# The queue that issues MoE 1's stores of the parts of x

## The chip, the cores and the metric

One Trainium2 chip, one core. The metric is the device time of one execution in microseconds (us), taken as the median over runs. The profile is one further execution, recorded by the hardware profiler; all times of day in the text are us from the start of its span.

## What is computed

The reference runs three layers in float32 on 2304 tokens of 512 features:

```python
attn_out = _attn_ref(**attn_kwargs)                  # attention with a memory term
x = attn_out.transpose(0, 2, 1, 3).reshape(2304, 512)
x = (silu(x @ w_gate) * (x @ w_val)) @ w_out         # MoE 1, d_ff = 1536
logits = x @ w_gate2; P = sinkhorn(exp(logits))      # MoE 2, 8 experts of 1024
out = sum_e P[:, e] * (relu(x @ w1[e]) @ w2[e])
```

The kernel makes each float32 product out of three products of float32r halves (high by high, high by low, low by high), and in MoE 2 and in part of MoE 1 it replaces eight block products by seven (Strassen-Winograd), which needs sums of blocks of x beside the blocks themselves.

## The kernel before

Time runs through attention (to about 340 us), MoE 1 (to about 670 us) and MoE 2 (to the end). MoE 1 takes the tokens in chunks of 512, 512, 512, 512 and 256. Chunks 0 and 1 go first; chunks 2 and 3 then go through their gates together in seven block products per slice of d_ff (`unit_gates`, L1045, called from the loop at L883, the "gate stage" below, from 424 to 587 us); from 587 to 670 us the last product of chunk 3 and all of chunk 4 follow (loop at L955, the "last stage").

As soon as a chunk of MoE 1's output stands in `x` (buffer name `xacc`), its seven parts for MoE 2 (four blocks and the sums T1 to T4) are made and kept in HBM, since MoE 2 reads each part again for every unit of weights. `parts` (L731) lists the seven, `parts_of` (L704) makes one in three steps, spread over three turns of a generator: ScalarE casts the block to its high half (L717, into a tile `xl`), VectorE subtracts to get the low half into the same tile (L720), and a DMA stores the tile of 512 KB to `xp` (L723). There are two `xl` tiles in the pool (L858), so the cast of part n+2 waits until the store of part n has landed. The chunk's logits (L670) use the same two tiles (cast L681, subtraction L683).

The parts of pairs 0 and 1 are made in the gate stage, those of pair 2 in the last stage, each time as work "aside" that the loop pulls one step at a time (`on`, L774). The parts of pair 3 and of the last 256 tokens are made in MoE 2's first microseconds (`last_parts`, L1460). Pair p has the stores xp_64 to xp_70 (p = 0), xp_71 to xp_77 (p = 1), xp_78 to xp_84 (p = 2).

All other DMAs run from the sync engine's queue (SP): in the gate stage per slice 1 MB of gate weights (`gw`, L654), 512 KB of output weights (`ws`, L654), two loads of 256 KB for the sums of weights (`hf`, L1025) and one store of 256 KB (`kh`, L899).

In the gate stage the seven products of a slice share PSUM tiles: `pc` accumulates four of them in a row, and between them ScalarE must copy the running value out (L1062, `hf<-pc`) before TensorE may add the next product. Between those products TensorE has two others (`pt`) and pieces of the output product of an earlier slice (`po`, spread by PIECES, L113).

The order in which each engine's instructions stand is set by the scheduling layer when the program is built: it walks through all instructions by readiness, so an instruction that is put on another queue changes the order around it on other engines too. Within its engine's queue an instruction is taken strictly in order, and what waits at the head holds all behind it.

Of the kernel before, what the change touches and what calls it, by code (L numbers as in the profile page):

```python
# [114 lines left out]
PAIRS2 = 4  # L115
# [17 lines left out]
def f32(ap):  # L133
    return ap.bitcast(F32)
# [26 lines left out]
class Kernel:  # L161
# [438 lines left out]
    def load_units(self):  # L600
# [14 lines left out]
        for n, (f, a) in enumerate(RAW):  # L615
# [5 lines left out]
            if a < 2:  # L621
                parts, kept = self.gw[f][:, :, a], self.keptg[f][:, :, a]
            else:
                self.ws[f] = self.wsp.tile([P, 2, 512], F32R, name="ws")
                parts, kept = self.ws[f], self.kepto[f]
# [15 lines left out]
            if a < 2:  # L641
                nc.sync.dma_start(self.keptw[f][:, a], w)
            nc.vector.tensor_sub(parts[:, 1], w, f32(parts[:, 0]))
            nc.sync.dma_start(kept, f32(parts))
            yield

# [54 lines left out]
        nc.vector.tensor_copy(sums, pl[:, :, 0])  # L701
        nc.vector.tensor_add(sums, sums, pl[:, :, 1])

    def parts_of(self, todo):  # L704


        nc, rest = self.nc, []
        for src, dst in [*todo, (None, None), (None, None)]:
            nxt = []
            for what in rest:  # L710
                nxt += what()
            rest = nxt
            if src is not None:
                src = src()
                t = self.xl.tile([P, 2, 512], F32R, name="xl")
                hi, lo = (t[:, n].rearrange("p (k t) -> p k t", k=2) for n in range(2))
                nc.scalar.copy(hi, src)  # L717

                def low(src=src, dst=dst, t=t, hi=hi, lo=lo):
                    nc.vector.tensor_sub(lo, src, f32(hi))  # L720

                    def store():
                        nc.sync.dma_start(dst, f32(t))  # L723
                        return []

                    return [store]

                rest.append(low)
            yield

    def parts(self, pair):  # L731

        t0, to = 2 * HT * pair, self.xparts[pair]
        q = {
            f"B{k + 1}{t + 1}": self.x[:, 2 * k:2 * k + 2, t0 + HT * t:t0 + HT * (t + 1)]
            for k in range(2) for t in range(2)
        }

        def total(name, a, b):
            def made():  # L740
                q[name] = self.tmpp.tile([P, 2, HT], F32, name="ws")
                self.nc.vector.tensor_sub(q[name], q[a], q[b])
                return q[name]

            return made

        plain = lambda name: lambda: q[name]
        yield from self.parts_of([
            (plain("B11"), to[0]), (total("T1", "B12", "B11"), to[3]), (total("T2", "B22", "T1"), to[2]),
            (plain("B21"), to[1]), (total("T3", "B22", "B12"), to[5]), (total("T4", "B21", "T2"), to[6]),  # L750
            (plain("B22"), to[4]),
        ])

    def moe1(self, last):


        nc, tc = self.nc, self.tc
        with ExitStack() as st, ExitStack() as waiting, ExitStack() as banks:
# [61 lines left out]
            def more(c, logits):  # L820
                t0, n = CHUNKS1[c]
                if logits:
                    yield from self.logits(pgv, "p0", self.xl, t0 // P, (t0 + n) // P)
                yield from self.parts(c)

            gws = self.stream(lambda: self.gwp, [P, 2, 2, 512], "gw", self.keptg * 2, 2)
            wss = self.stream(lambda: wsp0, [P, 2, 512], "ws", self.kepto * 2, 3)
# [31 lines left out]
            self.xwa_pool = ExitStack()  # L859
            self.xwa = pool("xwa", 3, self.xwa_pool)  # L860
            aside.append(more(0, True))


# [9 lines left out]
            for _ in ready:  # L873
                pass
            done(1, po)
            aside.append(more(1, False))


            banks.close()
            with ExitStack() as few:  # L880
                pc, pt = (pool(k, 2, few, space=PSUM) for k in ("pc1", "pt1"))
                po = new(n)
                for f in range(NF1):  # L883
                    weights(0, f)
                    todo = [(k, pend) for k in range(NK)] if f else []
# [29 lines left out]
            def both():  # L915

                steps = iter(lambda: next(self.prep0), 2)

                def behind():
                    while True:  # L920
                        with ExitStack() as order:
                            for ins in self.last_half:
                                order.enter_context(tc.issue_after(ins.ins))
                            if next(steps, self) is self:
                                return
                        yield

                weights0 = behind()
                for c in (1, 2):
                    t0, n = CHUNKS1[c]  # L930
                    for _ in self.logits(plog, "pl", self.xl, t0 // P, (t0 + n) // P):
                        yield next(weights0, None)
                for _ in self.parts(2):
                    yield next(weights0, None)
                for _ in weights0:
                    yield

            aside.append(both())
            h3p = pool("h3", 3, side="right")
            h3 = []  # L940
# [506 lines left out]
    def moe2(self):  # L1447
        nc, tc = self.nc, self.tc
        with ExitStack() as st:
# [9 lines left out]

            def last_parts():  # L1460

                yield from self.parts(PAIRS2 - 1)
                t0 = 2 * HT * PAIRS2
                yield from self.parts_of([
                    (lambda n=n: self.x[:, 2 * n:2 * n + 2, t0:NT], self.xparts[PAIRS2][n]) for n in range(2)
                ])

            def routing():
                for c in range(3, len(CHUNKS1)):
# [27 lines left out]
            right(0, 0)(0)  # L1497
            prep = self.prep0
            aside, pend, gate, nth = (last_parts(), routing()), [], 0, 0
            self.todo, self.now = [], 0  # L1500
            for u in range(UNITS):
# [110 lines left out]
```

## Time and profile before

| | |
|---|---|
| median of 3 runs | 2110.19 us (2109.23 to 2112.42) |
| the profiled execution | 2108.75 us, its span 2107.0 us |
| PE busy | 2065.8 us (98%) |
| DVE busy | 1718.9 us (82%) |
| ACT busy | 974.1 us (46%) |
| POOL busy | 523.0 us (25%) |
| DMA | 425.77 MB, mean 202 GB/s, all kernel transfers on one queue, q1 (59.9% of 16 engines' span) |

PE is TensorE, DVE is VectorE, ACT is ScalarE, SP the sync engine; `SPq` marks an instruction of SP's queue that issues a DMA. In a timeline row the bracket tells how long the engine stood idle before the row and what ended that. TensorE is the bound almost throughout, so what counts is where it stands idle; the page's slices show it below nine tenths only in the first.

### The profile page before, as it was taken

The numbers are of one execution on the slowest core, as the hardware profiler recorded it, in microseconds if no ns is written. First come the engines' busy times: TensorE is split into PE (matmuls) and PEld (weight loads), VectorE is DVE, ScalarE is ACT, GpSimd is POOL, SyncE is SP. The second block draws the span as 40 slices with busy tenths as digits, with TensorE's granted clock in tenths as the row PEclk, the third lists the DMA queues.
The fourth block names the chain that finished last, engine by engine and source line by source line (L and its number), as shares of the span: only waits on it lengthen the run. The fifth ranks groups of instructions, "written<-read, shape, count | busy, mean of one in ns | idle before, by whom it ended". The sixth has DMA issues, their size and how long they took to land.

```text
span 2107.0 us, 40598 instructions
## 1 busy us (share of the span) xinstructions
PE 2065.8 (98%) x15848; PEld 1904.7 (90%) x15848; DVE 1718.9 (82%) x3201; ACT 974.1 (46%) x1912; POOL 523.0 (25%) x458
## 2 busy tenths in 40 slices
PE   7999999999999999999999999999999999999999
PEld 5666787877889779999999999999999999999998
DVE  7899899674454578888888888988889888898887
ACT  7999543353333324444444444444444444444432
POOL 6888553000000032122121221212212122121210
PEclk9999999999999999999999999999999999999999
DMA  5342687375587837566475664755647556476564
GB/s 191 114 140 83 195 286 263 132 262 194 171 284 250 300 106 250 184 216 221 160 242 194 205 221 160 248 193 201 225 161 245 197 194 230 160 242 204 186 212 159
DMA packets 123359, 425.77 MB, mean 202 GB/s; under 512 B 13600, under 2 KB 13600, under 8 KB 120096
## 3 DMA queue, kind: packets, MB, share of 16 engines
q1 hardware_dynamic: 123168, 423.17, 59.9%
q8 instruction: 126, 2.06, 0.4%
q14 instruction: 65, 0.53, 0.1%
HBM read 374.36 MB, written 48.76 MB: 201 GB/s over the span
## 4 chain that ended last, share of the span: by engine, by line
PE 69%; DVE 11%; DMA 3%; issue 1%; ACT 1%; SPq 0%; DVEq 0%; ACTq 0%
PE pu L1433 16%; PE pc L1270 14%; PE pq L1433 11%; PE pt L1270 10%; PE po L546 5%; PE pt L1356 4%; PE p L546 3%; PE pc L546 3%; DVE m L1286 2%; DVE xacc L1439 2%; PE pt L546 2%; PE pq L546 2%; DMA xp<-xl 2%; DVE h L1255 1%; DVE h L1252 1%; DMA xr<-xp 1%
## 5 line engine op out<-in xcount | busy, mean ns | idle before, releaser
L1433 PE MATMUL pu<-xl,h 128*128 128x256 f32 x3240 | 424.8, 278 | 2.8 <-DVE xacc L1439 2.3
L1433 PEld LDWEIGHTS pu<-xl,h 128*128 128x128 f32 x3240 | 393.0, 188 | 7.2 <-DVE xacc L1439 4.0
L1270 PE MATMUL pc<-xr,w 128*128 128x256 f32 x3072 | 392.4, 277 | 4.9 <-DMA xr<-xp 3.4
L1270 PEld LDWEIGHTS pc<-xr,w 128*128 128x128 f32 x3072 | 369.1, 188 | 8.7 <-DMA xr<-xp 3.7
L1433 PE MATMUL pq<-xl,h 128*128 128x256 f32 x2430 | 316.9, 277 | 0.0
L1270 PE MATMUL pt<-xr,w 128*128 128x256 f32 x2304 | 294.1, 277 | 0.5 <-DMA xr<-xp 0.4
L1433 PEld LDWEIGHTS pq<-xl,h 128*128 128x128 f32 x2430 | 294.0, 188 | 0.3
L1254 ACT CAST h<-m 128x512 fp32r<-128x512 f32 (+1 forms) x345 | 190.3, 556 | 201.7 <-DVE m L1286 194.0
L1270 PEld LDWEIGHTS pt<-xr,w 128*128 128x128 f32 x2304 | 276.6, 188 | 1.8 <-issue 1.4
L1439 DVE SCALAR_TENSOR_TENSOR xacc<-pu,Pw,xacc 128x256 f32<-128x256 f32 x540 | 236.7, 474 | 38.7 <-PE pu L1433 38.6
L1277 ACT COPY m<-pc 128x512 f32<-128x512 f32 x192 | 112.1, 584 | 256.9 <-PE pc L1270 255.5
L1439 DVE SCALAR_TENSOR_TENSOR xacc<-pq,Pw,xacc 128x256 f32<-128x256 f32 x405 | 177.3, 473 | 47.1 <-PE pq L1433 47.1
L1255 DVE TENSOR_TENSOR h<-m,h 128x512 fp32r<-128x512 f32 (+1 forms) x345 | 207.0, 624 | 1.6
L1175 POOL TENSOR_TENSOR ws<-raw 128x512 f32<-128x512 f32 x60 | 80.8, 1358 | 502.7 <-DMA raw<-w 177.2
L1286 DVE SCALAR_TENSOR_TENSOR m<-m 128x512 f32<-128x512 f32 x240 | 187.0, 779 | 15.0 <-ACT m L1313 11.6
L1251 ACT ACTIVATE h<-m 128x512 fp32r<-128x512 f32 x192 | 121.4, 632 | 162.4 <-DVE m L1282 161.2
L1282 DVE TENSOR_TENSOR m<-pt,m 128x512 f32<-128x512 f32 x192 | 131.1, 683 | 57.5 <-ACT m L1277 51.4
L546 PE MATMUL p<-xs,gw 128*128 128x512 f32 (+1 forms) x864 | 171.0, 354 | 3.6 <-ACT hf L782 1.7
L546 PEld LDWEIGHTS p<-xs,gw 128*128 128x128 f32 x864 | 142.3, 188 | 30.7 <-DVE hf L783 2.8
L1252 DVE SCALAR_TENSOR_TENSOR h<-m,h 128x512 fp32r<-128x512 f32 x192 | 148.4, 773 | 7.6 <-ACT h L1251 7.2
L1162 POOL TENSOR_TENSOR w<-raw,w 128x512 fp32r<-128x512 f32 x15 | 38.6, 2574 | 435.3 <-ACT w L1161 435.3
L546 PE MATMUL po<-h,ws 128*128 128x512 f32 x576 | 144.6, 391 | 0.1
(229 smaller groups left out, 2943.0 us busy)
## 6 DMA issues: line engine op xcount, KB each, us to landing
xr<-xp SPq DMA_DIRECT2D x480, 512.0 KB, 4.1
raw<-w SPq DMA_DIRECT2D x64, 512.0 KB, 7.6
gw<-kg SPq DMA_DIRECT2D x24, 1024.0 KB, 7.1
graw<-gvo SPq DMA_DIRECT2D x36, 512.0 KB, 4.5
xp<-xl SPq DMA_DIRECT2D x30, 512.0 KB, 5.5
kg<-gw SPq DMA_DIRECT2D x24, 512.0 KB, 4.4
ws<-ko SPq DMA_DIRECT2D x24, 512.0 KB, 3.8
qk<-qkv SPq DMA_DIRECT2D x16, 640.0 KB, 4.9
```

The costliest lines, as they stand in the source:

```text
L546: self.nc.tensor.matmul(out, lhs[a], rhs[b], start=start and n == 0, stop=stop and n == 2, skip_group_check=shared)
L1251: nc.scalar.activation(hi, src, AF.Relu)
L1252: self.later(1, lambda: nc.vector.scalar_tensor_tensor(lo, src, 0.0, f32(hi), op0=ALU.max, op1=ALU.subtract))
L1254: nc.scalar.copy(hi, src)
L1255: self.later(1, lambda: nc.vector.tensor_sub(lo, src, f32(hi)))
L1270: self.marks[3] = nc.tensor.matmul(out[:, j * HT:(j + 1) * HT], w[:, a, j, k], x[:, b, k], start=start and j + k + n == 0, stop=k + n == 3 ...
L1277: self.marks[1] = nc.scalar.copy(t, src)
L1282: nc.vector.tensor_add(t, a, b)
L1286: relu = lambda out, a, b, op: nc.vector.scalar_tensor_tensor(out, a, 0.0, b, op0=ALU.max, op1=op)
L1356: nc.tensor.matmul(ph[:, j * HT:(j + 1) * HT], w[:, b, j, k], x[:, c, k], start=j + a + k + m == 0, stop=a + k + m == 4, skip_group_check= ...
L1433: nc.tensor.matmul(po[:, c], h[a][:, x, j, c * P:(c + 1) * P], w2[b][:, y, j], start=start and c + j + n == 0, stop=j + n == 3, skip_group ...
L1439: self.marks[2] = nc.vector.scalar_tensor_tensor(acc, po[:, c], self.Pw[:, at, e:e + 1], acc, op0=ALU.mult, op1=ALU.add)
```

## The change

`parts` and `parts_of` take the queue as an argument; MoE 1 passes ScalarE's, MoE 2 the sync engine's as before.

```diff
-    def parts_of(self, todo):
+    def parts_of(self, todo, queue):
...
                     def store():
-                        nc.sync.dma_start(dst, f32(t))
+                        queue.dma_start(dst, f32(t))
                         return []
...
-    def parts(self, pair):
+    def parts(self, pair, queue):
...
-        ])
+        ], queue)
...
-                yield from self.parts(c)
+                yield from self.parts(c, nc.scalar)
...
-                for _ in self.parts(2):
+                for _ in self.parts(2, nc.scalar):
...
-                yield from self.parts(PAIRS2 - 1)
+                yield from self.parts(PAIRS2 - 1, nc.sync)
...
-                ])
+                ], nc.sync)
```

21 of the 30 stores move (pairs 0 to 2), 9 stay (pair 3 and the last tokens). The orders of ACT, DVE, PE and SP differ in the gate stage's first 50 us, those of ACT, DVE and SP once more in the last stage; POOL's is the same.

ACT, second slice of the gate stage, before (L717 cast of a part, L802 cast of the gated values, L1062 copy of the running product, L1077 and L1088 the silu of the two token blocks):

```order
L717 CAST xl<-xacc 128x512
L1062 COPY hf<-pc 128x512
L717 CAST xl<-xacc 128x512
L802 CAST h<-sg 128x512
L1062 COPY hf<-pc 128x512
L1077 ACTIVATE sg<-hf 128x512
L717 CAST xl<-ws 128x512
L1062 COPY hf<-pc 128x512
```

The same place on ACT in the changed program:

```order
L717 CAST xl<-xacc 128x512
L723 DMA xp_70<-xl 128x1024
L723 DMA xp_68<-xl 128x1024
L802 CAST h<-sg 128x512
L1062 COPY hf<-pc 128x512
L717 CAST xl<-xacc 128x512
L717 CAST xl<-ws 128x512
L1077 ACTIVATE sg<-hf 128x512
L1062 COPY hf<-pc 128x512
L723 DMA xp_71<-xl 128x1024
L723 DMA xp_74<-xl 128x1024
L1062 COPY hf<-pc 128x512
```

Two stores now stand ahead of the cast and the copy, and the second copy stands behind both of the casts that wait for these two stores to land; before, one such cast stood between two copies.

ACT, third slice of the gate stage, in the changed program (L1040 casts the sums of weights, L681 the logits' blocks):

```order
L717 CAST xl<-ws 128x512
L1062 COPY hf<-pc 128x512
L1040 CAST ws<-ws 128x1024
L717 CAST xl<-ws 128x512
L723 DMA xp_76<-xl 128x1024
L1077 ACTIVATE sg<-hf 128x512
L723 DMA xp_77<-xl 128x1024
L717 CAST xl<-xacc 128x512
L1062 COPY hf<-pc 128x512
L723 DMA xp_75<-xl 128x1024
L1062 COPY hf<-pc 128x512
L681 CAST xl<-xacc 128x512 x2
```

The middle copy follows a cast that waits for xp_76, which was issued only three instructions earlier.

PE in that slice in the changed program (`pc<-xs,ws` is the second and the third product of the running sum, `pc<-ws` the fourth, and each of them waits for a copy L1062):

```order
L546 MATMUL pc<-xs,ws 128x512 x6
L546 MATMUL po_5317<-h,ws 128x512
L546 MATMUL po_5318<-h,ws 128x512 x2
L546 MATMUL po_5319<-h,ws 128x512 x2
L546 MATMUL po_5320<-h,ws 128x512 x2
L546 MATMUL pt<-xs,gw 128x512 x6
L546 MATMUL pc<-xs,ws 128x512 x6
L546 MATMUL pc<-ws 128x512 x6
```

Between the second product and the third TensorE has 13 other matmuls, between the third and the fourth none; before, there was one `po` piece or more between the third and the fourth in every slice but the first.

## Rows read from the trace of the kernel before

**Rows 1.** Busy time by stretch (us): PE, PEld, DVE, ACT, POOL; PEclk; DMA share; GB/s.

```profile
420.00:587.00 167.00, 162.54 (x709) 130.56 (x708) 95.16 (x165) 66.48 (x109) 1.53 (x2) 0.99 0.62 206
...
587.00:670.00 83.00, 83.00 (x561) 75.65 (x560) 38.08 (x73) 26.45 (x53) 0.00 (x0) 1.00 0.78 281
670.00:720.00 50.00, 45.00 (x304) 38.68 (x303) 31.44 (x54) 20.63 (x39) 0.00 (x0) 1.00 0.92 325
...
470.00:480.00 10.00, 6.91 (x29) 5.15 (x28) 4.21 (x10) 2.84 (x5) 0.00 (x0) 0.98 0.80 260
480.00:490.00 10.00, 10.00 (x39) 8.07 (x39) 5.95 (x11) 3.84 (x6) 0.00 (x0) 0.85 0.51 158
```

**Rows 2.** Timeline of the gate stage, PE: start, us, instruction, idle before it.

```profile
451.18 1.67 PE L546 MATMUL pc<-ws 128*128 128x512 f32 x6 [1.37 <-ACT hf L1062]
...
479.50 2.93 PE L546 MATMUL pc<-ws 128*128 128x512 f32 x6 [3.02 <-ACT hf L1062]
```

**Rows 3.** Timeline of the gate stage, ACT.

```profile
450.03 0.62 ACT L717 CAST xl<-ws 128x512 fp32r<-128x512 f32 x1 [3.51 <-DMA xp<-xl]
450.55 0.58 ACT L1062 COPY hf<-pc 128x512 f32<-128x512 f32 x1
...
478.35 0.62 ACT L681 CAST xl<-xacc 128x512 fp32r<-128x512 f32 x1 [6.05 <-DMA xp<-xl]
478.87 0.58 ACT L1062 COPY hf<-pc 128x512 f32<-128x512 f32 x1
```

**Rows 4.** The chain that ended last, gate stage: start, us, what.

```profile
468.29 10.04 DMA xp<-xl
...
487.31 1.36 PE pc L546 x6
```

**Rows 5.** Timeline of SP's queue at the slowest store.

```profile
465.73 0.32 SPq L654 DMA_DIRECT2D ws<-ko  x1
467.09 0.32 SPq L654 DMA_DIRECT2D gw<-kg  x1
468.29 0.32 SPq L723 DMA_DIRECT2D xp<-xl  x1
```

**Rows 6.** DMA view, 424 to 470 us: queue share; issues, KB each, median us to landing.

```profile
q1 hardware_dynamic: 3633, 12.33, 75.5%
...
xp<-xl SPq DMA_DIRECT2D x14, 512.0 KB, 3.7
```

**Rows 7.** The stores' line L723 over the whole span.

```profile
DMA to landing us min/median/max: 2.6/5.5/10.0
```

**Rows 8.** Groups by line, ACT, 420 to 587 us: busy us, mean ns, idle before.

```profile
L1062 ACT COPY hf<-pc 128x512 f32<-128x512 f32 x36 | 21.1, 587 | 55.4 <-PE pc L546 55.4
L1040 ACT CAST ws<-ws 128x1024 fp32r<-128x1024 f32 x12 | 12.6, 1053 | 15.8 <-PE pc L546 15.8
L1077 ACT ACTIVATE sg<-hf 128x512 f32<-128x512 f32 x12 | 7.6, 634 | 1.3 <-DVE hf L1067 0.7 <-DVE h L803 0.6
...
L717 ACT CAST xl<-ws 128x512 fp32r<-128x512 f32 x8 | 4.9, 619 | 5.9 <-DMA xp<-xl 3.5 <-PE p L698 2.4
```

**Rows 9.** Groups by line, 420 to 480 us, DVE's low halves.

```profile
L720 DVE TENSOR_TENSOR xl<-ws,xl 128x512 fp32r<-128x512 f32 x8 | 5.5, 684 | 2.8 <-ACT xl L717 2.8
```

**Rows 10.** DMA issues that touch xp: ns min/median/max, first and last start.

```profile
L1484 SPq DMA_DIRECT2D xr<-xp x480: 319/320/1336, 667.9 to 2074.8; - x160
L723 SPq DMA_DIRECT2D xp<-xl x30: 319/320/492, 424.6 to 712.0; - x30
```

**Rows 11.** Timeline of the last stage, ACT.

```profile
634.55 0.62 ACT L717 CAST xl<-ws 128x512 fp32r<-128x512 f32 x1 [2.67 <-DMA xp<-xl]
635.07 0.38 ACT L782 ACTIVATE sg<-p 128x256 f32<-128x256 f32 x1
```

**Rows 12.** Timeline of the last stage, PE.

```profile
630.98 3.10 PE L546 MATMUL p<-xs,gw 128*128 128x256 f32 x24
...
638.10 2.17 PE L546 MATMUL p<-xs,gw 128*128 128x256 f32 x17
```

## The prediction

> **What bounds the kernel now.** I read the page first (PE 98% busy), then the busy time by stretch, because a change to 21 stores can only matter where TensorE stands idle while they are made. The stores of pairs 0 and 1 lie in the gate stage, those of pair 2 in the last stage. In the gate stage PE is busy 162.54 of 167.00 us, so 4.46 us are idle [rows 1]. In the last stage it is busy 83.00 of 83.00 us: nothing to gain there [rows 1]. From 670 to 720 us it idles 5.00 us [rows 1], but those are MoE 2's first loads and the nine stores that stay on SP; the order there is the same in both programs, so I let it move along unchanged.
>
> The 4.46 us are next to all in two waits, 1.37 and 3.02 us, both before a `pc<-ws` product and both ended by the copy L1062 on ACT [rows 2]. The ACT timeline tells why that copy was late: it stands directly behind a cast into an `xl` tile that had waited 3.51 and 6.05 us for a store to land [rows 3]. The chain that ended last runs through that store: issued at 468.29, landed 10.04 us later [rows 4]. The second wait also costs clock: the granted clock is 0.98 from 470 to 480 us and 0.85 from 480 to 490 [rows 1], and the product after the wait takes 2.93 us against 1.36 for six matmuls at full rate [rows 2, 4]. Of the two levels, 2.4 and 1.2 GHz, that is about 3 us at the lower one after 3 us of idleness; the lost work is 10 x 0.02 + 10 x 0.15 = 1.7 us. So the **ceiling of any gain is 4.46 + 1.7 = 6.2 us**, 0.29% of the time.
>
> **The change, part by part.** *Removed from SP:* 21 issues of 0.32 us [rows 10]. SP only issues DMAs; its queue is never what PE waits for in the gate stage (both waits go to a landing, not to an issue). Worth nothing by itself.
>
> *Added to ACT:* the same 21 issues. No ACT issue is in the trace; the nearest rows are SP's issues, 0.32 us in the median, 0.49 at most for these stores and 1.34 at most for the loads of the same tiles [rows 10]. I take 0.32, since shape and size are the same: 6.7 us over two stages in which ACT is busy 66.48 of 167 and 26.45 of 83 us [rows 1]. That room covers them, unless one stands directly ahead of a copy that PE needs.
>
> *A new wait on ACT:* each store waits for its own low half (L720, 0.68 us [rows 9]) at the head of ACT's queue; cast 0.62 [rows 8] plus low half plus handover is 1.4 us from the cast's start. Where the store stands right behind the cast, about 0.7 us of ACT are lost; behind it are copies, silus and casts. In 11 of the 21 places it also waits for an older transfer on the semaphore that it reuses; these were issued some eight transfers, or over 10 us, earlier, which is as long as the slowest landing [rows 7], so I price that at nothing.
>
> *Moved:* the order. The cast of part n+2 still waits for the landing of part n, on the same ACT queue, with the copies behind it. What replaces the two waits of before has to be worked out from the orders of the changed program. I use six matmuls 1.36 us, that is 0.227 each [rows 4]; copy 0.59, L1077 0.63, cast 0.62, L1040 1.05 [rows 8]; low half 0.68 [rows 9]; and as time to landing 3.7 us, the median of the 14 stores of this stage [rows 6]. Its ends are 2.6, the shortest, and 5.5, the median of all 30 [rows 7].
>
> - Place A, second slice: from the issue of xp_68 to the end of the second copy lie landing 3.7, cast 0.62, L1077 0.63, copy 0.59, with handovers 5.6 us. PE has, from about 0.4 us after that issue, 6 + 3 + 6 + 4 = 19 matmuls, 4.3 us. It idles 0.9 us (0 at a landing of 2.6; 2.7 at 5.5).
> - Place B, third slice, the product shown in the order: from the first copy's end ACT has L1040 1.05, cast 0.62, xp_76, landing 3.7, cast 0.62, copy 0.59, with handovers 6.6 us; PE has 6 + 7 + 6 = 19 matmuls, 4.3 us. It idles 2.3 us (1.2; 4.1).
> - Place C: the first copy of that slice stands behind a cast that waits for xp_73, and the products before it end about when it does: 0.35 us (0; 1.5).
> - Place D: the third and the fourth product stand back to back, so PE waits one copy and a handover, 0.7 us at any landing time.
> - Places E and F: two silus L1088 behind two casts each, one pair waiting for xp_71 and xp_74, the other for xp_77 and xp_75: 0.35 and 0.4 us (0; 1.5 each).
>
> The sum is 5.0 us of idleness in place of 4.46, +0.5. The clock I leave as it was: B and D together are 3.0 us of idleness within some 4 us, like the 3.02 of before. Last stage: the silu L782 reads the `p` tile that PE needs again; before it ran at 635.07 although a cast ahead of it waited 2.67 us, and the next `p` began at 638.10 [rows 11, 12], so 3.0 less 0.8 us for L782 and the product on DVE, some 2 us, are room. In the new order the cast, its low half and the store xp_82 stand ahead of one silu; a landing of 3.7 us leaves the room just covering it, one of 5.5 us lacks 1.5 us. I take 0.3 us. Together **+0.8 us**: 2109.6 us against the profiled 2108.75 us (span 2107.0 and 1.75 us around it). The median of the runs is 1.44 us above the profiled one, so on that scale 2110.19 + 0.8 = 2111.0 us.
>
> **The rivals.** *Stores overtake the loads (faster).* On SP's queue a store stands behind the weights: the slowest one was issued 1.20 us after 1 MB of `gw` and 2.56 us after 512 KB of `ws` [rows 5] and took 10.04 us [rows 4], four times the shortest. If a store on ACT's queue no longer waits for loads issued ahead of it, landings come near 2.6 us: A, C, E and F vanish, B leaves 1.2 and D 0.7, 1.9 us in all, and no wait is long enough for the clock to fall. That gives 2110.2 + 1.9 - 6.2 = 2105.9 us. For it speak those rows; against it that the median of these 14 is already 3.7 and that the DMA engines carry 75.5% over this stretch [rows 6], so the bytes ahead must move anyway. The Trainium skill, "DMA: Bandwidth & Descriptors", section "Queues, rings and completion order", has a rule for it: the sync and the scalar engine own a row of rings each, and every DMA engine goes round-robin between the rows packet by packet. By that rule this rival is what happens; the slow store of the trace agrees with its other half, that one row is drained in order. No row has two queues, so I give the rival 0.20. The section "Issuing engines are not separate DMA queues" of the same page speaks the other way: queues of several engines share the same DMA engines, and only issue time is saved; by that the sum would be that of an unchanged landing time, mine.
>
> *Pairs of stores hold up ACT (slower).* In the new order the stores of the gate stage mostly stand in pairs (xp_70 and 68, 71 and 74, 73 and 72), so that the second has 512 KB more ahead of it, and in A the copy waits for the second. If the landing that counts is 5.5 us, the places give 2.7 + 4.1 + 1.5 + 0.7 + 1.5 + 1.5 = 12.0 us instead of 4.46, and the last stage 1.5: +9.0, or 2119 us. It decides from a landing of about 4.5 us, where the sum passes +4.2. For it: two casts of before waited about that long for a store, 3.51 and 6.05 us [rows 3]; against it: the median landing of the 14 is 3.7 us [rows 6]. Chance 0.25. An issue on ACT of up to 1.34 us [rows 10] would add about 1 us at each of four stores ahead of a needed copy and end in the same band; I count it there.
>
> **How the numbers follow.** What a measurement of this kernel can tell from no change is about 0.2%, 4.2 us. My forecast, landings between 3 and 4.5 us, gives -2 to +4 us and holds 0.55, all within 0.2%; its own range is 2108 to 2114 us. The first rival, -4.3 us, just beyond the bound, has 0.20, the second 0.25. The range reaches to 2105 below, the first rival, whose floor is 2110.2 - 6.2 = 2104.0, and to 2118 above, most of the second; that leaves out 2 in 10 at most.
>
> **What would show it right or wrong.** A second DMA queue with 21 transfers, landing in 3 to 4.5 us. In the gate stage PE idles about 5 us; the longest wait is before a `pc<-xs,ws` product, ended by L1062 behind a cast that waited for xp_76, some 2.3 us; one of 0.7 us stands before a `pc<-ws`. ACT's issues take 0.32 us. The last stage stays at about 83 us, MoE 2 as it was. I am wrong if the landings are under 3 us and PE idles under 2.5 us (first rival), if they are over 4.5 us and PE idles over 9 (second), or if the difference lies after 670 us.

## The result, and the profile after

The changed kernel is slower: **2126.36 us** median of 6 runs (2122.58 to 2129.53) against 2109.54 us before (6 runs, 2107.80 to 2112.42), a ratio of **1.0077, 95% interval 1.0063 to 1.0091**. Forecast was 2111.0 us within 2105 to 2118. The profiled execution took 2126.56 us, its span 2124.8 us, 17.8 us more than the span of before. Among the runs below, one execution of e10 (9304 us) and one of the kernel before (2136.71 us) stand far off the rest and are left out of the ratios.

Busy time by stretch of the changed kernel, with the columns of [rows 1]:

```profile
420.00:587.00 167.00, 157.37 (x674) 125.92 (x673) 91.80 (x159) 63.42 (x104) 1.53 (x2) 0.98 0.59 198
450.00:460.00 10.00, 4.52 (x11) 3.47 (x11) 2.55 (x5) 3.69 (x7) 0.00 (x0) 0.72 0.62 223
460.00:470.00 10.00, 10.00 (x42) 8.04 (x41) 6.13 (x9) 4.39 (x8) 0.00 (x0) 0.94 0.74 246
587.00:670.00 83.00, 79.86 (x509) 70.41 (x508) 39.94 (x73) 26.95 (x53) 0.00 (x0) 0.98 0.83 291
650.00:660.00 10.00, 7.45 (x39) 6.27 (x40) 4.55 (x8) 4.09 (x8) 0.00 (x0) 0.83 0.81 261
```

TensorE now idles 9.63 us in the gate stage (4.46 before) and 3.14 us in the last stage (none before). All of it is in five waits. Timeline, PE, with the idle time in brackets as in [rows 2]:

```profile
455.58 2.93 PE L546 MATMUL pc<-xs,ws 128*128 128x512 f32 x6 [5.48 <-ACT hf L1062]
474.72 1.66 PE L546 MATMUL pc<-xs,ws 128*128 128x512 f32 x6 [1.36 <-ACT hf L1062]
477.06 1.66 PE L546 MATMUL pc<-ws 128*128 128x512 f32 x6 [0.68 <-ACT hf L1062]
482.19 1.43 PE L546 MATMUL pc<-xs,gw 128*128 128x512 f32 x5 [2.12 <-ACT sg L1088]
652.55 4.63 PE L546 MATMUL po<-h,ws 128*128 128x512 f32 x12 [3.13 <-ACT h L802]
```

The first four are the places A, B, D and F of the prediction, in that order; the fifth is in the last stage, at a place that it did not price. The product behind the first wait took 2.93 us, the one behind the fifth 4.63 us where the same 12 matmuls take 2.88 elsewhere in this stage: that is the lower clock, and the granted clock is 0.72 and 0.83 in those stretches.

How ScalarE came to be late at place A, its timeline:

```profile
443.23 0.62 ACT L717 CAST xl<-xacc 128x512 fp32r<-128x512 f32 x1 [0.17 <-DMA xp<-xl]
443.29 2.45 ACTq L723 DMA_DIRECT2D xp<-xl  x2
...
446.31 0.59 ACT L1062 COPY hf<-pc 128x512 f32<-128x512 f32 x1
452.12 0.62 ACT L717 CAST xl<-xacc 128x512 fp32r<-128x512 f32 x1 [5.22 <-DMA xp<-xl]
453.91 0.62 ACT L717 CAST xl<-ws 128x512 fp32r<-128x512 f32 x1 [1.18 <-DMA xp<-xl]
...
454.96 0.57 ACT L1062 COPY hf<-pc 128x512 f32<-128x512 f32 x1
```

xp_70 is issued at 443.29 and xp_68 at 445.42 (the row's x2); two casts in a row wait for them; behind the casts stands the copy that TensorE has wanted since 450.1. SP had issued 1 MB of `gw` 0.41 us ahead of the first of the two, and the chain that ended last goes through the second store:

```profile
442.88 0.32 SPq L654 DMA_DIRECT2D gw<-kg  x1
```

```profile
445.42 8.47 DMA xp<-xl
...
455.58 2.93 PE pc L546 x6
```

The last stage, ACT and SP: two stores with a load of `gw` between them, a cast that waits 7.14 us, and behind it L802, which `po` needs:

```profile
642.15 0.33 ACTq L723 DMA_DIRECT2D xp<-xl  x1
642.62 0.38 ACT L782 ACTIVATE sg<-p 128x256 f32<-128x256 f32 x1
643.47 0.33 ACTq L723 DMA_DIRECT2D xp<-xl  x1
650.14 0.62 ACT L717 CAST xl<-xacc 128x512 fp32r<-128x512 f32 x1 [7.14 <-DMA xp<-xl]
650.66 0.40 ACT L802 CAST h<-sg 128x256 fp32r<-128x256 f32 x1
```

```profile
642.44 0.32 SPq L654 DMA_DIRECT2D gw<-kg  x1
```

The landings of the 14 stores of the gate stage, then of the seven of the last stage:

```profile
DMA to landing us min/median/max: 2.6/3.7/8.8
...
DMA to landing us min/median/max: 2.9/7.6/9.2
```

The median of the gate stage is what it was [rows 6], 3.7 us. The two stores for which TensorE waits are the slowest of the 14 (8.8 and 8.5).

**Where the 17.8 us are.** MoE 2's first matmul starts at 688.57 us, 13.25 us later than before (675.32). Of these, 1.2 us arose before the gate stage (its first `pc` product starts at 432.04 against 430.82, though nothing is changed there; the granted clock of the first 100 us was 0.95 in this execution and 0.98 in that of before); 5.2 are idleness in the gate stage; 1.7 are clock there, estimated from the stretches as in the prediction (10 x 0.28 + 10 x 0.06 = 3.4 us against 1.7); the last stage has 3.1 us of idleness and, by the same estimate, 10 x 0.17 = 1.7 of clock. That adds up to 12.9. The other 4.5 us lie in MoE 2, whose program is the same but for the semaphores of its first loads; they are taken up below.

### The profile page after: what moved, and what is told of

Read it like the earlier page. It is cut to its first block, busy times and chain, and to the rows that moved or that the text cites. A ratio compares the mean times of both kernels' runs of the same rounds, so it can differ in the third digit from the quotient of the medians.

```text
span 2124.8 us, 40586 instructions
## 1 busy us (share of the span) xinstructions
PE 2074.3 (98%) x15848; PEld 1910.0 (90%) x15848; DVE 1719.0 (81%) x3201; ACT 973.9 (46%) x1912; POOL 521.8 (25%) x458
## 4 chain that ended last, share of the span: by engine, by line
PE 66%; DVE 11%; DMA 5%; issue 1%; ACT 1%; SPq 0%; ACTq 0%; DVEq 0%
PE pu L1433 15%; PE pc L1270 13%; PE pq L1433 10%; PE pt L1270 9%; PE po L546 5%; PE pt L1356 4%; DMA xr<-xp 3%; PE pc L546 3%; PE p L546 2%; DMA xp<-xl 2%; PE pt L546 2%; DVE xacc L1439 2%; DVE m L1286 2%; PE pq L546 2%; DVE h L1255 1%; DVE h L1252 1%
## 5 line engine op out<-in xcount | busy, mean ns | idle before, releaser
L1270 PE MATMUL pc<-xr,w 128*128 128x256 f32 x3072 | 393.4, 277 | 7.2 <-DMA xr<-xp 5.7
L1270 PEld LDWEIGHTS pc<-xr,w 128*128 128x128 f32 x3072 | 369.6, 188 | 11.9 <-issue 4.5
L1270 PE MATMUL pt<-xr,w 128*128 128x256 f32 x2304 | 294.5, 277 | 0.8 <-DMA xr<-xp 0.7
L1270 PEld LDWEIGHTS pt<-xr,w 128*128 128x128 f32 x2304 | 276.9, 188 | 2.2 <-issue 1.4
```

The costliest lines, as they stand in the source:

```text
L1270: self.marks[3] = nc.tensor.matmul(out[:, j * HT:(j + 1) * HT], w[:, a, j, k], x[:, b, k], start=start and j + k + n == 0, stop=k + n == 3 ...
```

## The experiments

Ratios are to the kernel before on the same chip, over all the runs of both and not of the two medians, with 95% intervals; its median there is 2107 to 2108 us. "MoE 2 starts" is the start of the first L1270 matmul in the profile (675.3 before). It still holds what one execution lost or won before the gate stage, where nothing is changed but in e15 (its loads): the first `pc` product starts between 428.8 and 434.2 us, and latest where the granted clock of the first 100 us was lowest (0.93 in e13, against 1.00 in e15 and 0.98 before). So the last column gives the time from that first `pc` product to MoE 2. It holds all that the stores can move before MoE 2, and is free of that scatter and of MoE 2's own. It is that of one execution each.

| run | median us | ratio (interval) | MoE 2 starts, us | first `pc` to MoE 2, us |
|---|---|---|---|---|
| kernel before | 2109.54 | | 675.3 | 244.5 |
| changed kernel | 2126.36 | 1.0077 (1.0063 to 1.0091) | 688.6 | 256.5 |
| changed kernel again (e14) | 2124.18 | 1.0073 (1.0058 to 1.0087) | 689.2 | 258.7 |
| e1: gate stage alone on ACT | 2119.47 | 1.0052 (1.0035 to 1.0069) | 682.4 | 251.4 |
| e2: last stage alone on ACT | 2113.43 | 1.0018 (1.0004 to 1.0032) | 677.9 | 248.0 |
| e3: on POOL | 2123.66 | 1.0067 (1.0050 to 1.0085) | 685.0 | 253.7 |
| e4: ACT, no cast waits for a landing | 2105.70 | 0.9983 (0.9972 to 0.9995) | 670.4 | 237.8 |
| e5: SP, casts placed by hand | 2102.58 | 0.9976 (0.9965 to 0.9987) | 668.0 | 237.7 |
| e6: ACT, casts and stores placed | 2115.85 | 1.0039 (1.0026 to 1.0052) | 682.0 | 250.2 |
| e7: POOL, casts placed | 2104.39 | 0.9990 (0.9979 to 1.0000) | 670.5 | 240.7 |
| e8: ACT, last stage placed | 2120.65 | 1.0057 (1.0042 to 1.0071) | 683.2 | 254.1 |
| e9: ACT, casts alone placed | 2109.86 | 1.0000 (0.9989 to 1.0011) | 671.1 | 241.1 |
| e10: SP, casts in pairs | 2112.42 | 1.0010 (0.9997 to 1.0022) | 673.1 | 242.5 |
| e11: SP, order of the changed kernel | 2119.77 | 1.0053 (1.0040 to 1.0066) | 680.5 | 251.6 |
| e12: ACT, order of before | 2121.31 | 1.0062 (1.0047 to 1.0077) | 685.0 | 252.6 |
| e13: POOL, order of before | 2120.03 | 1.0051 (1.0035 to 1.0068) | 684.4 | 250.2 |
| e15: as e13, big loads on POOL too | 2110.39 | 1.0016 (1.0007 to 1.0025) | 681.3 | 251.5 |

### Which stage, and is it the wait for a landing?

e1 and e2 give one stage each back to SP, e3 puts the stores on GpSimd's queue:

```diff
# e1
-                for _ in self.parts(2, nc.scalar):
+                for _ in self.parts(2, nc.sync):
# e2
-                yield from self.parts(c, nc.scalar)
+                yield from self.parts(c, nc.sync)
# e3
-                yield from self.parts(c, nc.scalar)
+                yield from self.parts(c, nc.gpsimd)
...
-                for _ in self.parts(2, nc.scalar):
+                for _ in self.parts(2, nc.gpsimd):
```

e4 leaves out the 21 stores of the parts themselves and stores a finished block of x in their place, as many bytes each, right behind the part's own cast, so that no `xl` tile waits for a store:

```diff
-                        queue.dma_start(dst, f32(t))
+                        with self.tc.issue_after(cast.ins):
+                            queue.dma_start(dst, self.x[:, 0:2, 0:512])
```

> Only the 14 stores of pairs 0 and 1 (gate stage) are issued from ScalarE; pair 2's seven go back to the sync engine. Theory A (copies that TensorE needs stand on ScalarE behind casts that wait for stores issued together with 1 MB loads): the gate stage costs what it cost in the changed kernel, 8.3 us (the last stage began at 592.37 in place of 584.06), the last stage nothing: about 2118 us. Theory B (any transfer on a second queue slows all of them, in MoE 2 too): 2118 plus the 4.5 us that MoE 2 took longer, about 2122. Theory C (the last stage is what hurts): under 2113.

> Only pair 2's seven stores (last stage) are issued from ScalarE; the 14 of the gate stage go back to the sync engine. Theory A: the gate stage idles 4.5 us as before, the last stage loses 4.9 us (a cast L802 behind a cast that waits for a store, then TensorE at the lower clock): about 2114.5 us. Theory B: 4.5 us more in MoE 2, about 2119. Theory C: 2120 or over.

> All 21 stores are issued from GpSimd's queue, which does next to nothing in these stages; ScalarE carries no store. Theory A: the stores are on a second queue as well, but ScalarE's order has one cast between two copies as before; 2107 to 2113 us, TensorE idle 3 to 6 us in the gate stage. Theory B (a second queue makes landings longer): landings in the gate stage over 5 us in the median, TensorE idle over 8 us, 2118 us or more. If a store alone no longer waits for the weights ahead of it, landings near 2.6 us and about 2105.

> As the changed kernel, but each of the 21 stores on ScalarE reads a block of x that is complete, in place of the xl tile (the parts that it should store are left out), and is issued right behind its own cast; the bytes, the queue and the number of issues stay, and no cast waits for a landing. Theory A: TensorE idles under 1.5 us in the gate stage and not at all in the last one, no clock is lost: 2103 to 2108 us. If the issues on ScalarE and what they wait for themselves hold up the copies, 2115 us or more although no cast waits for a store.

e1 and e2 came out as the first theory had it, 0.52% and 0.18%: two thirds of the loss are the gate stage's. (e1's interval alone doesn't set theory A, 8.3 us, apart from theory B, 12.8 us; its trace does, with the waits of the changed kernel in the gate stage and a MoE 2 of 1434.1 us.) e4 is 0.17% faster than before, although its 21 issues on ScalarE took longer (0.52 us instead of 0.33) and its transfers too (9.6 us in the median). Busy time of its gate stage:

```profile
420.00:590.00 170.00, 170.00 (x766) 138.30 (x765) 100.59 (x174) 68.45 (x113) 1.54 (x2) 1.00 0.65 220
```

TensorE idles nowhere there. So the whole loss ahead of MoE 2, and before's 4.46 us, hang on casts that wait for a landing; the issues themselves cost next to nothing (what an issue waits for its low half went with the parts, so e4 does not test that). e3 was a miss: I expected 2107 to 2113 us of a queue that burdens nobody, and it is 0.67% slower. Either a second queue costs even where ScalarE carries no store, or the order does that changed with it here too; e13 below separates them.

### Does it go away when the casts stand elsewhere?

e5 to e9 set ScalarE's order by hand. In the gate stage a step of the parts is taken only behind a slice's first and last copy, so that a cast mostly meets a store 7 us old or more; in the last stage the casts stand behind L802:

```diff
-                        on()
+                        if at in (0, 4):
+                            with tc.issue_after(self.kept.ins):   # the last copy L1062
+                                on()
...
-                for _ in self.parts(2):
-                    yield next(weights0, None)
+                todo = self.parts(2)
+                while True:
+                    with tc.issue_after(self.last_half[0].ins):   # L802
+                        if next(todo, self) is self:
+                            break
+                    yield next(weights0, None)
```

e5, e6 and e7 are this on SP, ACT and POOL; e8 is the changed kernel with the second hunk alone; e9 is e6 with the casts alone held, not the stores.

> The queue of before (sync engine), but ScalarE's order is set by hand: in the gate stage one step of the parts is issued only behind the first and the last of a slice's three copies L1062, so that a cast meets a store that was issued some 10 us earlier; in the last stage the casts stand behind the cast L802. Theory A (what costs is where the casts that wait for a landing stand on ScalarE): TensorE idles under 1 us in the gate stage, not at all in the last, no clock lost: 2102 to 2106 us.

> The same order set by hand, with the 21 stores on ScalarE's queue as in the changed kernel. Theory A: next to the same as with the sync engine's queue, 2102 to 2107 us, under 2 us idle in the gate and the last stage together. Theory B (the second queue or ScalarE's issues cost by themselves): 2112 us or more.

> The same order set by hand, with the 21 stores on GpSimd's queue. Theory A: 2102 to 2107 us, as the other two. Theory B: 2112 us or more.

> The changed kernel with the order set by hand in the last stage alone: the casts of pair 2 stand behind L802. Theory A: the 3.1 us of idleness before the po product and the lower clock behind it go, the gate stage keeps its 8.3 us: 2117 to 2121 us, as with the gate stage alone on ScalarE. If a store on ScalarE in the last stage costs wherever the cast stands: 2124 or more.

> As the run with the order set by hand and the stores on ScalarE, but only the casts are held behind the copies and behind L802; the stores, which that order had also held back by a copy, are issued as soon as their low half stands. Theory A (only where the casts stand against the landing matters, not the queue): 2102 to 2107 us, under 2 us idle in the gate and the last stage together. Theory B (issues and stores on ScalarE cost by themselves): 2111 us or more, with idleness before products that follow a copy behind a store.

e5 is **faster than both kernels**, 0.24%: TensorE is busy throughout the gate stage, and MoE 2 starts 7.3 us earlier than before. Of these 0.5 us come from ahead of the gate stage; the rest is a little over the ceiling of 6.2 us that the prediction read.

```profile
420.00:590.00 170.00, 170.00 (x769) 138.03 (x768) 99.48 (x172) 67.90 (x113) 1.53 (x2) 1.00 0.65 225
```

e7 gains less on another queue, 0.10%, with 1.7 us of idleness left, so a second queue is nearly harmless once no cast is close behind a store. e8 costs 0.57% where the changed kernel costs 0.77%, inside what I expected. e6 was a miss of my own making: the hold also held the stores, which on ScalarE then stood one copy later, and the next cast met them about 4 us old. With the stores let go (e9), the gate stage idles not at all; what is left is 2.6 us in the last stage, 2.29 of them before L802 (expected under 2 us in all). Its time is like that of before, between what the two theories had, so it is a miss too; up to MoE 2 it is 3.4 us faster than before, and that its MoE 2 took 1436.8 us here is open, as below. e9 shows another thing about ScalarE's queue: there a store has a place in the order, and that place must be chosen too.

### The order or the queue?

In the changed kernel both are new. e10 tries the order roughly (each copy behind all casts traced so far, so that casts come in pairs, on SP). e11 and e12 do it exactly: from the two built programs I took the order of ScalarE's, VectorE's and TensorE's instructions where they differ (stretches of 337 in all, of which 269 stand at another place) and chained them, so that e11 is the changed kernel's order with the stores on SP, e12 before's order with the stores on ACT, e13 the same on POOL, whose orders on these three engines are row by row those of before:

```diff
+def in_order(nc, tc):
+    by = {i.name: i for i in nc.cur_bb.bb.instructions}
+    for row in STANDS:
+        row = [by[f"I-{n}"] for n in row.split()]
+        for a, b in zip(row, row[1:]):
+            tc.add_manual_dep(b, a.name, ...)        # issue order alone
...
         body(tc, *args)
+        in_order(nc, tc)
```

> The reverse: the queue of before (sync engine), but in the gate stage each copy L1062 is issued behind all casts of parts traced so far, so that two casts in a row stand ahead of a copy, as in the changed kernel. Theory A: the stores land no faster there, so TensorE idles 8 us or more in the gate stage and the time is 2114 to 2122 us, without any store on another queue. If the queue is what made the changed kernel slow: within 3 us of before, 2107 to 2111 us.

> The stores on the sync engine's queue as before, but ScalarE's, VectorE's and TensorE's instructions are chained into the exact order of the changed kernel. If the order alone is the cause: 2120 to 2128 us, with TensorE's waits of 5 and 2 us in the gate stage and 3 us before the po product in the last. If the queue alone is the cause (landings next to loads that were issued after the store too, issues on ScalarE): 2107 to 2111 us. Half and half: 2112 to 2118.

> The stores on ScalarE's queue as in the changed kernel, but the other instructions of ScalarE, VectorE and TensorE are chained into the order of before. If the order alone is the cause: within 3 us of before. If the queue alone: 2120 or more. If both: 2112 to 2118.

> The stores on GpSimd's queue, the other engines chained into the order of before: a second queue without an issue on ScalarE. If a second queue makes the landings that count longer, as much as with ScalarE's queue in this order; if issues and their waits on ScalarE cost, about as before, 2105 to 2111 us.

> The changed kernel once more, on the same chip as these three. All theories: 2122 to 2130 us and the same waits at the same places; if the 4.5 us that its MoE 2 was longer are chance, its MoE 2 (from the first matmul of MoE 2 to the end of the span) may be anywhere between 1431 and 1438 us.

e10 missed: 0.10%, not distinct from before. Pairs of casts as such don't cost much on SP. e11, the exact order, costs 0.53%, just under what I had for "the order alone"; e12, the queue alone, 0.62%, and e13 0.51%. So both cost. By the times they don't add up (0.73 to 0.77% for both together); by the profiles, from the first `pc` product to MoE 2, they about do: 7.1 us for the order, 5.7 (e13) and 8.1 (e12) for the queue, 12.0 and 14.2 for both. Why the two counts differ is open; the profiled execution of e11 is its fastest, 2115.57 us. Place A in e11, and its landings in the gate and in the last stage:

```profile
449.83 1.66 PE L546 MATMUL pc<-xs,ws 128*128 128x512 f32 x6 [2.94 <-ACT hf L1062]
```

```profile
DMA to landing us min/median/max: 2.6/3.6/6.0
...
DMA to landing us min/median/max: 3.7/5.0/6.0
```

The order is the changed kernel's, but the wait at A is 2.94 us and not 5.48, and no store takes over 6.0 us, where the changed kernel's run to 8.8 and 9.2. (The third wait that I expected, 3 us before the `po` product, came as 2.65 us before a `p` product.) Two reasons show in the queues. First, on SP xp_70 was issued before the `gw` load, as soon as its low half stood; on ScalarE a cast that waited stood ahead of it, its low half was ready at 442.0 (L720 ran from 441.32 for 0.69 us), it went out at 443.29, and `gw` had gone at 442.88. Second, in the last stage a load behind a store slows it less on the store's own queue than on another. SP's queue in e11, last stage; then POOL's and SP's in e13:

```profile
641.12 0.90 SPq L723 DMA_DIRECT2D xp<-xl  x2
642.12 0.87 SPq L654 DMA_DIRECT2D gw<-kg  x1
```

```profile
639.77 0.53 POOL L723 DMA_DIRECT2D xp<-xl  x1 [3.99 <-DVE xl L720]
```

```profile
640.88 0.32 SPq L654 DMA_DIRECT2D gw<-kg  x1
```

The two of e11 landed after 5.6 and 6.0 us with a megabyte right behind them in their queue. The one of e13, 1.1 us ahead of the megabyte on the other queue, took 8.3, and the changed kernel's at 642.15, 0.29 us ahead, 8.0. It is not so of every store: in the gate stage of e12 two that went out 0.58 and 0.79 us ahead of `gw` on the other queue landed after 2.9 and 3.9 us; less was under way there.

Nor did a queue of its own take a store past a load that was issued just ahead of it. The DMA view of the changed kernel at place A, where xp_70 went out at 443.29, first to 447.80 us, then to 452 us (packets, MB, share of 16 engines):

```profile
q1 hardware_dynamic: 116, 0.94, 82.4%
q10 hardware_dynamic: 1, 0.00, 0.2%
```

```profile
q10 hardware_dynamic: 262, 0.97, 57.1%
q1 hardware_dynamic: 260, 0.53, 36.1%
```

For 4.5 us the stores' queue (q10) moved next to nothing while the sync engine's (q1) moved 0.94 MB; after that both moved. The rule of the Trainium skill that I gave 0.20 (page "DMA: Bandwidth & Descriptors", section "Queues, rings and completion order": the DMA engines go in turn between the rows) agrees with the second stretch and not with the first; why the stores' queue started so late is open. What I read from the rule, that a store would no longer wait for what is ahead on the other queue, did not hold here.

e13 shows a third reason, on the sync engine. In before, two stores at 455.60 and 456.80 landed in 3.1 and 3.2 us, with the next load of `gw` only behind them in SP's queue; freed of the stores, SP issues that load first. SP's queue before, then SP's and POOL's in e13:

```profile
455.60 1.52 SPq L723 DMA_DIRECT2D xp<-xl  x2
...
458.42 0.51 SPq L654 DMA_DIRECT2D gw<-kg  x1
```

```profile
459.10 0.32 SPq L654 DMA_DIRECT2D gw<-kg  x1
```

```profile
460.27 0.53 POOL L723 DMA_DIRECT2D xp<-xl  x1 [3.66 <-DVE xl L720]
461.47 0.53 POOL L723 DMA_DIRECT2D xp<-xl  x1 [0.67 <-DVE xl L720]
```

These took 8.8 and 9.4 us. In e12's last stage it is the same: `gw` went at 640.64, the two stores at 640.71 and 642.02, and they landed after 7.9 and 8.6 us.

### One queue again, on GpSimd

e15 is e13 with the big loads in the same queue as the stores:

```diff
-                self.nc.sync.dma_start(f32(tiles[-1]), sources[len(tiles) - 1])
+                self.nc.gpsimd.dma_start(f32(tiles[-1]), sources[len(tiles) - 1])
```

> As the run with the stores on GpSimd's queue in the order of before, with one change: the loads of gw and ws (L654) are issued from GpSimd's queue too, so that stores and big loads stand in one queue again, one behind the other. If two queues that share the DMA engines are what makes the stores that count land late: landings beside a load come back to about 6 us from 7 to 9, and the time to 2105 to 2113 us. If GpSimd's queue as such is slow: 2118 us or more, as without this change.

The time lies where I expected it, 0.16% above before, but the trace does not give that to the stores: from the first `pc` product to MoE 2 e15 takes 251.5 us, e13 250.2 and before 244.5. The landings came back in the last stage alone. It is whole again:

```profile
590.00:670.00 80.00, 80.00 (x535) 72.67 (x535) 39.38 (x73) 26.93 (x54) 13.32 (x26) 1.00 0.81 301
```

There a pair's first store, issued 1.4 us ahead of `gw` in the same queue, landed in 5.6 us, where in e13 it took 8.3 with the load on the other queue:

```profile
638.96 0.54 POOL L723 DMA_DIRECT2D xp<-xl  x1 [1.47 <-DVE xl L720]
640.35 0.53 POOL L654 DMA_DIRECT2D gw<-kg  x1 [0.85 <-PE p L546]
```

The gate stage is not whole: it idles 9.7 us (7.8 in e13; 2.3 of the 9.7 come at 571 us, after the last of these stores), with landings up to 9.9, and in this queue the load stands ahead of the same two stores:

```profile
454.87 0.53 POOL L654 DMA_DIRECT2D gw<-kg  x1 [0.82 <-PE pt L546]
455.77 0.54 POOL L723 DMA_DIRECT2D xp<-xl  x1 [0.37 <-DVE xl L720]
```

They took 9.3 and 9.9 us. So in one queue a store waits for what stands ahead of it, and which one that is has to be chosen; whether GpSimd's queue as such costs something, e15 doesn't tell. Of the 11.9 us between the two profiled executions, 4.4 lie before the gate stage and 8.8 in MoE 2, while the two stages are 1.2 us longer. MoE 2 took 1426.5 us in this one, the shortest of all; what moved it is open.

**MoE 2's 4.5 us** in the changed kernel I can't give to the change. From its first matmul to the end of the span MoE 2 took 1431.7 us before, 1436.2 in the changed kernel and 1433.8 in its repeat; with the stores on SP 1433.6 (e5), 1436.6 (e10) and 1433.3 (e11); on other queues 1431.4 (e2) to 1437.9 (e7), and 1426.5 in e15. The difference lies in waits for `xr` loads here and there. A cost of 2 to 3 us in the mean would not show in these; that stays open.

## Why the prediction was wrong

- **What bounds the kernel, the ceiling**: right. The waits are where casts meet landings, and e5 got the ceiling (6.7 us from the first `pc` product to MoE 2).
- **Issues on ScalarE** (0.32 us each, no cost): right, 0.33 us in the median and 0.44 at most, and e4 shows no cost.
- **The places**: A, B, D and F hold the gate stage's idleness, in the order that the programs' rows showed; C and E vanished, and D is as said (0.68 for 0.7). B came out smaller (1.36 for 2.3), by errors that partly cancel: xp_76 was issued 0.35 us after the first copy's end and not 1.7, it took 5.27 us and not 3.7, and TensorE began the 19 matmuls 1.0 us after that copy, since five `po` matmuls still stood ahead. That is luck of the sizes; the rows stand below the list.
- **The step that failed: "as time to landing 3.7 us, the median of the 14 stores of this stage".** The median was 3.7 again, but the two stores at A took 8.8 and 8.5 us, and the one at F 6.1. My own formulas then give A 0.9 + (8.5 - 3.7) = 5.7 us, measured 5.48, and F 0.4 + (6.1 - 3.7) = 2.8, measured 2.12. The pair at A was issued just behind a load of 1 MB on the other queue and moved next to nothing for 4.5 us; what was under way, not the median, set its landing. The trace of before had such a store, at 10.04 us [rows 4], and I kept it out of the range.
- **"Unchanged landing time"** on another queue: wrong for the stores that count, right for those that stand alone. In the same order SP landed the two in 2.8 and 5.9 us.
- **The last stage** (0.3 us, at L782): the wrong instruction. L782 got through at 642.62; the cast behind it, moved ahead of L802, waited for the first of the pair (7.96 us to its landing) and cost 3.1 us and 1.7 of clock.
- **The clock** "I leave as it was": by the estimate from the stretches it lost 5.1 us in both stages for 1.7.
- **"MoE 2 as it was"**: it took 4.5 us longer in the profile, and whether that is the change's stays open.
- **The second rival**, pairs of stores that hold up ACT, is what happened, though not by the pair's own 512 KB alone: xp_70, with no store of its pair ahead of it, took 8.8 us behind the load. Its 9.0 us were short of the 16.8 in part because it took 5.5 us for the landing that counts, and its end bounded the range. **The first rival** fell: the median landing stayed 3.7 us, and the two that TensorE waits for longest took 8.8 and 8.5.

Place B, PE's row of the five matmuls that stood ahead, then ACT's of xp_76 and of the cast and the copy behind it:

```profile
467.76 1.30 PE L546 MATMUL po<-h,ws 128*128 128x512 f32 x5
```

```profile
468.27 0.33 ACTq L723 DMA_DIRECT2D xp<-xl  x1
...
473.56 0.62 ACT L717 CAST xl<-xacc 128x512 fp32r<-128x512 f32 x1 [3.65 <-DMA xp<-xl]
474.09 0.58 ACT L1062 COPY hf<-pc 128x512 f32<-128x512 f32 x1
```

## What to carry to other kernels

Where a wait hangs on one transfer, price it by the landing of that transfer next to what is issued around it, not by the median of its group. One DMA queue is also a priority list: a short store ahead of a big prefetch was served first (5.6 and 6.0 us in e11). On a queue of its own, even an idle engine's, it lost that place: the prefetch went out ahead of it (8.8 and 9.4 us in e13), or slowed it from behind (8.3). Before moving DMAs, look at what waits for their landing on an engine that works in order: placing those few instructions (0.24% faster here, on the old queue) did what no change of queue did by itself.

## What the runs showed that I had not expected

- Putting 21 DMAs on another queue put 269 instructions of three engines at another place, and that order alone, with the old queue, cost 0.53%.
- A 512 KB store that was issued 0.41 us after a 1 MB load of another queue moved next to nothing for 4.5 us and took 8.8, where the shortest takes 2.6.
- In the first 100 us, where nothing is changed, the granted clock was 0.93 to 1.00 from one execution to the next, and the gate stage began up to 5 us apart.
- An issue of these stores took 0.53 us on GpSimd, 0.33 on ScalarE and 0.32 on the sync engine; none of the three was what TensorE waited for.
